# Two MLP layers of a fused attention and MLP kernel: an instruction order written by hand is replaced by one that a list scheduler in the source works out

## The chip, the cores and the metric

One core of one Trainium2 chip runs the whole kernel. The metric is the time of one execution on the device in microseconds (us); the number for a kernel is the median of its runs.

## The reference, cut to what matters

The inputs are float32 arrays: q, k and v of shape (2, 12, 448, 64), and the weights of two MLPs. With `n = 2 * 448 = 896` tokens and a model width of 768 it computes

```
x   = causal_attention(q, k, v)                   # laid out as 896 x 768
x   = (silu(x @ w_gate) * (x @ w_val)) @ w_out    # w_gate, w_val: 768 x 1536
h   = x @ w_in                                    # w_in: 768 x 2048
out = (h * clip(h + 3, 0, 6) / 6) @ w_out2
```

## The kernel before, in words

**The work and its stages.** Four stages follow one another on TensorE: attention, the gate and value layer of the first MLP with its product (here "the f loop"), the layer `w_out` of that MLP, and then the two layers of the second MLP. The weights reach the chip as 64-bit numbers in pairs of 32-bit words, and every 128-column tile of them is turned into float32 on the chip: one ScalarE instruction (`sloped`, line 147) and two on VectorE (`to_float`, line 137: a shift, then an or that joins the low word, which the profile calls TENSOR_SCALAR and SCALAR_TENSOR_TENSOR). Every operand is then split into a high part (a ScalarE copy) and a low part (a subtraction, line 154 for weights, 250 for the tokens), and `mm3` (line 246) makes each product out of three matmuls: high by high, high by low, low by high.

**The f loop.** There are twelve tiles f of 128 columns of `w_gate` and `w_val`. Tile 0 is computed directly for both batches (`first`, line 682, 72 matmuls). Tiles 1 to 11 use seven products instead of eight: each tile's gate and value weights and the two batches of tokens form a 2 by 2 block product in Winograd's scheme. It needs four sums of weight halves (s1 to s4), seven weight pieces, each with its high and low part (a11, s3, s2, s1, a12, a22, s4), the token combinations t1 to t4 made once after attention (line 250), and per f 63 matmuls in seven products in the four PSUM banks x, z, y, w. VectorE joins them with five additions (u2, u3, v2, z, w), ScalarE copies x (p1) and applies Silu twice, and VectorE multiplies gate by value twice (`gate`, line 642). For f below 4 the gated result is split at once; for f from 4 on it is kept in float32 and split later (`halves`, line 669), since no buffers are free until the tokens of attention have been read for the last time.

**What sets the order.** TensorE, VectorE, ScalarE and GpSimd each execute their queue in order. After attention a program-order flag is set for the three vector engines (`on`, line 677) and for TensorE (`on_pe`, line 768); from there to the end of the kernel each engine's queue is the order of the source. That order is written by hand: `chores` (line 722) is a table that says which steps of the next weight tiles stand behind which of the seven products, with special tables for f = 1 and f = 2 and additions for the last f; `slot_work` (line 761) issues them. In the rows of f = 1 the weight tile f + 1 is made whole and tile f + 2 is loaded and turned into float32. The hand-written order also fixes the engine of each subtraction: for f below 3 the low parts of s2, a12 and s4 are on VectorE, all others on GpSimd; the sums s1 and s3 are on GpSimd, s2 and s4 on VectorE; the splits of t3 are on GpSimd, of t2 and t4 on VectorE. The low parts of the `w_out` units (line 158) are on GpSimd, and their loads run two units ahead (line 206). Weight loads go through SyncE's queue into two raw buffers.

Of the kernel before, what the change touches and what calls it, by code (L numbers as in the profile page):

```python
# [23 lines left out]
RAW = 2  # L24
WS = 6
# [5 lines left out]
PLAIN = 1  # L31
EARLY = 4
# [8 lines left out]
class InOrder:  # L41
# [4 lines left out]
    def __getattr__(self, name):  # L46
        call = getattr(self.engine, name)

        def issue(*args, **kw):
            ins = call(*args, **kw)  # L50
            return self.tc.keep_in_program_order(ins) if self.on else ins

        return issue


@with_exitstack
def tile_attention_glu_mlp(
# [517 lines left out]
    def mlps():  # L575
# [13 lines left out]
        (ta, tag_a), (tb, tag_b), (sg, tag_c) = (pair_tile(f"tmp{i}", F32) for i in range(3))  # L589
        s12, tag_s = slot([128, 2, HD, 128], F32, "s12")  # L590

        def operands(f):

            got, fl = {}, {}

            def load(i):
                got["raw", i] = load_raw(cols((w_gate, w_val)[i], f), KD, 128)

            def number(i, step):
                if step == 0:  # L600
                    fl[i] = ring_tile("w", [128, KD, 128], F32, "wgv"[::2][i])
                w = fl[i]
                to_float(w, got["raw", i], (step,))
                fl.update({("a11", "a21")[i]: w[:, :HD], ("a12", "a22")[i]: w[:, HD:]})

            def s1():
                pool.tensor_tensor(out=s12[:, 0], in0=fl["a21"], in1=fl["a22"], op=ALU.add)
                fl["s1"] = s12[:, 0]

            def s3():  # L610
                pool.tensor_tensor(out=fl["a21"], in0=fl["a11"], in1=fl["a21"], op=ALU.subtract)
                fl["s3"] = fl["a21"]

            def s2():
                vec.tensor_tensor(out=s12[:, 1], in0=fl["s1"], in1=fl["a11"], op=ALU.subtract)
                fl["s2"] = s12[:, 1]

            def s4():
                vec.tensor_tensor(out=fl["a12"], in0=fl["a12"], in1=fl["s2"], op=ALU.subtract)
                fl["s4"] = fl["a12"]  # L620

            def piece(name):
                t = got[name] = ring_tile("ws", [128, 2, HD, 128], F32R, name)
                split_w(t[:, 0], t[:, 1], fl[name], vec if f < 3 and name in ("s2", "a12", "s4") else pool)

            todo = {"load1": lambda: load(0), "load2": lambda: load(1)}
            todo.update({n + str(j): lambda i=i, j=j: number(i, j) for i, n in enumerate(("wg", "wv")) for j in (0, 1)})
            todo.update({"s1sum": s1, "s2sum": s2, "s3sum": s3, "s4sum": s4})
            todo.update({n: lambda n=n: piece(n) for n in ("s3", "a11", "s2", "s1", "a12", "a22", "s4")})
            return got, todo  # L630

        def product(ps, a, xk, first, last):
            mm3(
                ps,
                [(a[:, 0, k], a[:, 1, k], t[:, 0], t[:, 1]) for k, (t, _) in enumerate(xk)],
                first=first, last=last, shared=True,
            )

        lent["w"] = [free.pop() for _ in range(W_SLOTS)]
        g1 = {}  # L640

        def gate(f, b, out_ps, in0, in1, step=None):

            whole_f, hi, lo = g1[f]
            if whole_f is not None:
                vec.tensor_tensor(out=whole_f[0][:, BATCH[b]], in0=in0, in1=in1, op=ALU.mult)
                return
            if step != 1:
                vec.tensor_tensor(out=out_ps, in0=in0, in1=in1, op=ALU.mult)
            if step != 0:  # L650
                split(hi[0][:, BATCH[b]], lo[0][:, BATCH[b]], out_ps)

        def g_tiles(f):
            if f < EARLY:
                g1[f] = None, whole(F32R, f"gh{f}"), whole(F32R, f"gl{f}")
            else:
                g1[f] = whole(F32, f"g{f}"), None, None

        ops, todo = {}, {}
        for f in range(PLAIN, K1):  # L660
            ops[f], todo[f] = operands(f)

        def do(f, *names):
            for n in names:
                if f < K1:
                    for part in (n + "0", n + "1") if n in ("wg", "wv") else (n,):
                        todo[f][part]()

        def halves(*fs):
            for f in fs:  # L670
                src, tag = g1[f][0]
                hi, lo = whole(F32R, f"gh{f}"), whole(F32R, f"gl{f}")
                split_w(hi[0], lo[0], src, vec if f < EARLY + 3 or f % 2 else pool)
                g1[f] = None, hi, lo
                free.append(tag)

        on.append(1)
        ws = [made[u] for u in range(2)]
        used[0] += 2
        g_tiles(0)  # L680

        def first(b):

            got = []
            for wh, wl in ws:
                t, n = bank("mm")
                got.append((t[:, :S], n))
                mm3(
                    got[-1][0],
                    [(wh[:, k], wl[:, k], x1[b][k][0][:, 0], x1[b][k][0][:, 1]) for k in range(KD)],  # L690
                )
            idle.extend(n for _, n in got)
            return [t for t, _ in got]

        got = first(0)
        do(1, "load1", "load2", "wg")
        do(2, "load1")
        for h in range(HD):
            split_x(3, h, pool)
        act.activation(out=sg[:, 0], in_=got[0], func=AF.Silu)  # L700
        do(1, "wv")
        do(2, "load2")
        do(1, "s1sum", "s3sum")
        for h in range(HD):
            split_x(2, h, vec)
        do(1, "a11", "s2sum")
        for h in range(HD):
            split_x(4, h, vec)
        later = got[1]
        got = first(1)  # L710
        act.activation(out=sg[:, 1], in_=got[0], func=AF.Silu)
        do(1, "s3", "s2", "s1")
        free.extend(x1[1][h][1] for h in range(HD))
        free.extend(tag for _, tag in sums + more_sums)

        b11, b21, b22 = x1[0][:HD], x1[0][HD:], x1[1][HD:]
        t1, t2, t3, t4 = ([xs[k, h] for h in range(HD)] for k in (1, 2, 3, 4))

        def give(*lists):
            free.extend(tag for l in lists for _, tag in l)  # L720

        def chores(f):

            n = f + 1
            if f == 1:
                return {
                    0: [(1, "a12"), (2, "wg"), (3, "load1")],
                    1: [(1, "s4sum", "a22", "s4"), (2, "wv"), (3, "load2")],
                    2: [(2, "s1sum", "s3sum", "a11")],
                    3: [(2, "s2sum", "s3", "s2"), lambda: gate(0, 0, later, later, sg[:, 0], 0)],  # L730
# [194 lines left out]
```

## Time and profile before

| what | value |
|---|---|
| median of 3 runs | 628.6 us (628.02 to 628.69) |
| the profiled execution | 629.06 us, its span 627.3 us |
| attention, first matmul of the f loop at | 118.26 us |
| f = 1 starts, the layer `w_out` starts | 134.43 us, 302.42 us |
| last two layers | to the end of the span |

The page gives the busy time of each engine over the span, and the span in forty slices with each engine's busy tenths and TensorE's granted clock. A timeline row gives start, duration, engine, instruction, and in brackets how long the engine had stood idle and which instruction released it. "mm" is a PSUM bank, "a" and "s" are weight pieces, "t" token combinations, "x" the tokens, "w" and "v" the float32 gate and value tiles, "tmp" the buffers for u2, u3, v2, p1 and the Silu results. Almost every instruction stands on line 50, the helper that sets the program order, so rows are told apart by tile.

### The profile page before, as it was taken

What the parts mean: (1) busy time and instruction counts of PE and PEld (TensorE: products, weight loads), DVE (VectorE), ACT (ScalarE), POOL (GpSimd) and SP (SyncE); (2) the same over time, 40 slices, a digit from 0 to 9 for tenths busy, and PEclk for the clock granted to TensorE, in tenths of its full rate; (3) what the DMA queues carried; (4) which work ended last, traced back from release to release, by engine and by line L of the source; (5) the groups of instructions that cost most, each with busy time, mean ns of one, the idle gap of its engine ahead of it and who ended that gap; (6) DMA issues with size and microseconds to landing.
All of it is one profiled execution on the core that took longest, in us unless ns stands there. A gap on an engine that the chain in (4) does not pass through costs nothing.

```text
span 627.3 us, 9422 instructions
## 1 busy us (share of the span) xinstructions
PE 598.3 (95%) x3519; PEld 551.8 (88%) x3519; DVE 380.4 (61%) x713; ACT 289.6 (46%) x522; POOL 277.3 (44%) x214
## 2 busy tenths in 40 slices
PE   8999999987598999998999999999999999999997
PEld 5999999876477899998888889998889999999997
DVE  6888999897888777755753333455555556215201
ACT  5687778573544445434533223454555553213200
POOL 4566675274567887873323222222232224213300
PEclk9999999999999999999799999999999999999999
DMA  9555545243343433323134333333334346515102
GB/s 181 131 132 134 133 102 149 78 123 101 106 147 109 143 100 101 115 88 99 52 101 150 101 101 100 101 100 102 102 111 134 107 106 197 151 64 175 53 0 89
DMA packets 83920, 70.16 MB, mean 112 GB/s; under 512 B 35233, under 2 KB 79777, under 8 KB 83873
## 3 DMA queue, kind: packets, MB, share of 16 engines
q1 hardware_dynamic: 83872, 69.55, 38.4%
q8 instruction: 28, 0.46, 0.3%
q14 instruction: 20, 0.16, 0.1%
HBM read 61.73 MB, written 2.75 MB: 103 GB/s over the span
## 4 chain that ended last, share of the span: by engine, by line
PE 70%; DVE 13%; POOL 7%; issue 4%; ACT 4%; DMA 0%; SPq 0%; POOLq 0%; DVEq 0%; ACTq 0%
PE mm L50 56%; PE pv L480 5%; PE sc L409 4%; POOL s L50 4%; PE tp L452 3%; DVE w L50 3%; DVE v L50 3%; POOL a L50 2%; DVE mm L50 1%; PE tr L334 1%; DVE tmp L50 1%; POOL v L50 1%; DVE s L50 1%; ACT w L50 1%; DVE e L422 1%
## 5 line engine op out<-in xcount | busy, mean ns | idle before, releaser
L50 POOL TENSOR_TENSOR wlo<-w,whi 128x768 fp32r<-128x768 f32 (+1 forms) x47 | 85.7, 1824 | 232.5 <-ACT whi L50 199.1
L50 ACT CAST whi<-w 128x768 fp32r<-128x768 f32 (+1 forms) x47 | 38.6, 821 | 99.7 <-DVE w L50 92.6
L50 PE MATMUL mm<-whi,g2l 128*128 128x384 f32 x224 | 74.8, 334 | 0.0
L50 PE MATMUL mm<-whi,g2h 128*128 128x384 f32 x224 | 74.8, 334 | 0.0
L50 PE MATMUL mm<-wlo,g2h 128*128 128x384 f32 x224 | 74.8, 334 | 0.0
L480 PE MATMUL pv<-v,et 112*112 112x65 f32 x480 | 73.5, 243 | 0.8 <-DVE et L458 0.8
L50 DVE TENSOR_SCALAR w<-w 128x768 uint32<-128x768 uint32 (+1 forms) x58 | 50.8, 876 | 38.3 <-ACT w L50 36.0
L50 PE MATMUL mm<-x2h,wlo 128*128 128x384 f32 (+1 forms) x192 | 69.9, 364 | 0.0
L50 PE MATMUL mm<-x2l,whi 128*128 128x384 f32 (+1 forms) x192 | 69.8, 364 | 0.0
L50 PE MATMUL mm<-x2h,whi 128*128 128x384 f32 (+1 forms) x192 | 69.6, 362 | 0.0
L480 PEld LDWEIGHTS pv<-v,et 112*112 112x112 f32 x480 | 65.5, 177 | 2.2 <-DVE et L458 1.0
L50 PE MATMUL mm<-t,s 128*128 128x448 f32 x297 | 62.6, 366 | 2.8 <-DVE gl L50 1.8
L452 PE MATMUL tp<-ident,e 112*112 112x112 f32 x240 | 61.1, 260 | 2.3 <-ACT e L432 2.2
L50 PEld LDWEIGHTS mm<-t,s 128*128 128x128 f32 x297 | 55.6, 188 | 8.2 <-DVE gl L50 2.2
L432 ACT ACTIVATE e<-e,m 112x336 f32<-112x336 f32 (+1 forms) x96 | 48.7, 530 | 20.9 <-DVE m L422 20.6
L50 DVE SCALAR_TENSOR_TENSOR w<-raw,w 128x768 uint32<-128x768 uint32 (+1 forms) x58 | 57.0, 983 | 1.9
L50 PE MATMUL mm<-gl,whi 128*128 128x384 f32 (+1 forms) x144 | 52.9, 367 | 0.0
L50 PE MATMUL mm<-gh,wlo 128*128 128x384 f32 (+1 forms) x144 | 52.9, 367 | 0.0
L50 PE MATMUL mm<-gh,whi 128*128 128x384 f32 (+1 forms) x144 | 52.7, 366 | 0.0
L50 ACT ACTIVATE w<-raw 128x768 f32<-128x768 f32 (+1 forms) x58 | 51.6, 890 | 0.7 <-DMA raw<-in_moe_w_out_dram 0.7
L50 PE MATMUL mm<-x,a 128*128 128x448 f32 x198 | 44.2, 367 | 3.8 <-ACT tmp L50 2.0
L50 PEld LDWEIGHTS mm<-x,a 128*128 128x128 f32 x198 | 37.0, 188 | 7.6 <-ACT tmp L50 2.4
(119 smaller groups left out, 1312.3 us busy)
## 6 DMA issues: line engine op xcount, KB each, us to landing
raw<-in_moe_w_out_dram SPq DMA_DIRECT2D x28, 768.0 KB, 4.3
raw<-in_moe_w_in_dram SPq DMA_DIRECT2D x16, 768.0 KB, 4.5
raw<-in_moe_w_gate_dram SPq DMA_DIRECT2D x12, 768.0 KB, 4.2
raw<-in_moe_w_val_dram SPq DMA_DIRECT2D x12, 768.0 KB, 4.3
kn<-in_k_dram SPq DMA_DIRECT2D x24, 112.0 KB, 2.8
qn<-in_q_dram SPq DMA_DIRECT2D x24, 112.0 KB, 2.8
v<-in_v_dram SPq DMA_DIRECT2D x12, 224.0 KB, 3.2
out_dram<-ob SPq DMA_DIRECT2D x14, 192.0 KB, 1.8
```

The lines of the kernel that those rows point to most:

```text
L50: ins = call(*args, **kw)
L334: nc.tensor.transpose(tr[:, c * C : (c + 1) * C], n[:, c].rearrange("p j d -> p (j d)"), ident[:C, :C])
L409: nc.tensor.matmul(sp[:C, o : o + w], t["qq"][:, j, c * C : (c + 1) * C], t[("kk", "k2")[i]][:, j, 0:w], start=(i == 0), stop=(i == 1),)
L422: nc.vector.tensor_tensor_reduce(out=es, in0=sp[:C, o : o + w], in1=mask[:, S - w :], op0=ALU.add, op1=ALU.min, scale=-SCALE, scalar=3.0e3 ...
L432: nc.scalar.activation(out=es, in_=es, func=AF.Exp, scale=-1.0, bias=m[:, x : x + 1])
L452: nc.tensor.transpose(tp[:C, at - lo : at - lo + C], e[:, at : at + C], ident[:C, :C])
L480: nc.tensor.matmul(box["o"][:, qc, :], et[:, at : at + C], vt[:, j, c, :], start=(c == 0), stop=(c == qc))
```

## The change

The table of chores is gone. The f loop, the splits of the gated results, the layer `w_out` and the weights of the first two units after it are written down as operations of a `Plan`, each with a cost per engine in microseconds and with what it reads and writes, buffers included. `Plan.run` gives each operation a due time, worked backwards from a TensorE that never waits, and then places them: at each step the engine that can start earliest takes, among the operations ready for it, the one due first. TensorE's and SyncE's order stays that of the source. The result is the order in which the instructions are issued. The sums s1 to s4 and the low parts of weight pieces, of token combinations and of the late gated results may go to VectorE or GpSimd, whichever the plan finds free first; the low parts of the `w_out` units are on VectorE alone. Program order is enforced from plan time 9 (TensorE 15), and the flags are cleared behind the plan, so the last two layers are ordered by the framework's own scheduler. The numbers of matmuls, of conversions, of splits and of loads are unchanged. The core of the diff (removed lines left out except in `gate`):

```diff
 PLAIN = 1
+PINNED = 9.0
+START = {"act": 5.6, "vec": 7.9, "pool": 7.0, "pe": 0.0, "sp": 0.0}
+LAG = {"act": 0.15, "vec": 0.15, "pool": 0.15, "pe": 0.25, "sp": 2.4}
 EARLY = 4
...
+class Spot:
+    def __init__(self, make=None, place=None, real=None, ready=0.0):
+        self.make, self.place, self.real, self.ready, self.after = make, place, real, ready, set()
...
+class Plan:
+    def __init__(self):
+        self.ops, self.uses, self.on_place = [], {}, {}
+    def op(self, where, call, reads=(), writes=()):
+        i, before, ready = len(self.ops), set(), 0.0
+        for writing, spots in ((False, reads), (True, writes)):
+            for s in spots:
+                spot, part = s if isinstance(s, tuple) else (s, None)
+                if spot not in self.uses:
+                    self.uses[spot] = []
+                    old = self.on_place.get(spot.place)
+                    if old is not None:
+                        spot.after = {j for _, j, _ in self.uses[old]}
+                    if spot.place is not None:
+                        self.on_place[spot.place] = spot
+                before |= spot.after
+                ready = max(ready, spot.ready)
+                for p, j, w in self.uses[spot]:
+                    if (w or writing) and (p is None or part is None or p == part):
+                        before.add(j)
+                self.uses[spot].append((part, i, writing))
+        before.discard(i)
+        self.ops.append((where, call, before, ready))
+    def run(self, emit):
+        ops, n = self.ops, len(self.ops)
+        after = [[] for _ in range(n)]
+        for i, (_, _, before, _) in enumerate(ops):
+            for j in before:
+                after[j].append(i)
+        clock = 0.0
+        due = [None] * n
+        for i, (where, _, _, _) in enumerate(ops):
+            if "pe" in where:
+                due[i] = clock
+                clock += where["pe"]
+        for i in reversed(range(n)):
+            for j in after[i]:
+                t = due[j] - min(c + LAG[e] for e, c in ops[i][0].items())
+                due[i] = t if due[i] is None else min(due[i], t)
+            if due[i] is None:
+                due[i] = clock
+        left = [len(ops[i][2]) for i in range(n)]
+        at = [ops[i][3] for i in range(n)]
+        free_at = dict(START)
+        pe_order = [i for i in range(n) if "pe" in ops[i][0]]
+        sp_order = [i for i in range(n) if "sp" in ops[i][0]]
+        waiting = {i for i in range(n) if not left[i]}
+        placed = []
+        while waiting:
+            best = None
+            for e in free_at:
+                if e in ("pe", "sp"):
+                    line = pe_order if e == "pe" else sp_order
+                    mine = [line[0]] if line and line[0] in waiting else []
+                else:
+                    mine = [i for i in waiting if e in ops[i][0]]
+                if not mine:
+                    continue
+                t = max(free_at[e], min(at[i] for i in mine))
+                i = min((i for i in mine if at[i] <= t), key=lambda i: (due[i], i))
+                key = (t, due[i], ops[i][0][e], i, e)
+                if best is None or key < best:
+                    best = key
+            t, _, cost, i, e = best
+            waiting.discard(i)
+            free_at[e] = t + cost
+            if e in ("pe", "sp"):
+                (pe_order if e == "pe" else sp_order).pop(0)
+            placed.append((t, len(placed), i, e))
+            for j in after[i]:
+                left[j] -= 1
+                at[j] = max(at[j], t + cost + LAG[e])
+                if not left[j]:
+                    waiting.add(j)
+        assert len(placed) == n
+        for t, _, i, e in sorted(placed):
+            emit(t, e, ops[i][1])
+        self.placed = sorted(placed)
...
+        def parts_of(src, hi, lo, size, both=True):
+            (s, s_part, s_ap), (h, h_part, h_ap), (l, l_part, l_ap) = src, hi, lo
+            plan.op(
+                {"act": 0.1 + size * 0.00098},
+                lambda e: e.copy(h_ap(h()), s_ap(s())), reads=[(s, s_part)], writes=[(h, h_part)],
+            )
+            where = {"vec": 0.08 + size * 0.0012}
+            if both:
+                where["pool"] = 0.1 + size * 0.0027
+            plan.op(
+                where,
+                lambda e: e.tensor_tensor(
+                    out=l_ap(l()), in0=s_ap(s()), in1=h_ap(h()).bitcast(F32), op=ALU.subtract
+                ),
+                reads=[(s, s_part), (h, h_part)], writes=[(l, l_part)],
+            )
...
+        def gate(f, b, bank_, in0, in1):
 
             whole_f, hi, lo = g1[f]
+            mid = lambda t: t[:, BATCH[b]]
+            m = {"vec": 0.63}
             if whole_f is not None:
-                vec.tensor_tensor(out=whole_f[0][:, BATCH[b]], in0=in0, in1=in1, op=ALU.mult)
+                combine(m, at(whole_f, b, mid), in0, in1, ALU.mult)
                 return
-            if step != 1:
-                vec.tensor_tensor(out=out_ps, in0=in0, in1=in1, op=ALU.mult)
-            if step != 0:
-                split(hi[0][:, BATCH[b]], lo[0][:, BATCH[b]], out_ps)
...
+            s1, s2 = at(s12, 0, nth(0)), at(s12, 1, nth(1))
+            either = {"vec": 0.65, "pool": 1.2}
+            out = {}
+            def piece(name, src):
+                t = ring_spot("ws", [128, 2, HD, 128], F32R, name)
+                parts_of(src, at(t, 0, nth(0)), at(t, 1, nth(1)), HD * 128)
+                out[name] = t
+            combine(either, s1, a21, a22, ALU.add)
+            piece("a11", a11)
+            combine(either, a21, a11, a21, ALU.subtract)
+            piece("s3", a21)
+            combine(either, s2, s1, a11, ALU.subtract)
+            piece("s2", s2)
+            piece("s1", s1)
+            piece("a12", a12)
+            combine(either, a12, a12, s2, ALU.subtract)
+            piece("a22", a22)
+            piece("s4", a12)
+            return out
...
+            products(x, a["a11"], b11, True)
+            plan.op(
+                {"act": 0.54}, lambda e, x=x: e.copy(p1[2](ta()), tok(x())), reads=[x], writes=[p1[:2]]
+            )
+            products(z, a["s3"], tk[3], True)
+            products(y, a["s2"], tk[2], True)
+            combine(add, u2, Y, p1, ALU.add)
+            combine(add, u3, Z, u2, ALU.add)
+            products(w, a["s1"], tk[1], True)
+            combine(add, v2, W, u3, ALU.add)
+            products(x, a["a12"], b21, False)
+            silu(at(sg, 0, nth(0)), x)
+            products(z, a["a22"], tk[4], False)
+            combine(add, Z, Z, u2, ALU.add)
+            gate(f, 0, z, Z, at(sg, 0, nth(0)))
+            products(w, a["s4"], b22, False)
+            combine(add, W, W, u2, ALU.add)
+            silu(at(sg, 1, nth(1)), w)
+            gate(f, 1, w, v2, at(sg, 1, nth(1)))
+            idle.extend((nx, ny, nz, nw))
...
+        later = [unit(units[used[0] + i][0]) for i in range(AHEAD)]
+        by = {"act": act, "vec": vec, "pool": pool, "pe": ten, "sp": nc.sync}
+        def emit(t, engine, call):
+            if t >= PINNED and not on:
+                on.append(1)
+            if t >= PINNED + 6 and not on_pe:
+                on_pe.append(1)
+            call(by[engine])
+        plan.run(emit)
+        on.clear()
+        on_pe.clear()
+        made.extend((hi(), lo()) for hi, lo in later)
...
```

## Rows read from the trace of the kernel before

**Rows 1.** The profile's page: engine totals and forty slices of the span

```profile
PE 598.3 (95%) x3519; PEld 551.8 (88%) x3519; DVE 380.4 (61%) x713; ACT 289.6 (46%) x522; POOL 277.3 (44%) x214
...
PE   8999999987598999998999999999999999999997
...
PEclk9999999999999999999799999999999999999999
```

**Rows 2.** Waits of TensorE's matmuls, 118 to 300 us: total, times, longest

```profile
PE mm L50 <- DVE tmp L50: 10.6, 6, 3.1
...
PE mm L50 <- ACT gh L50: 2.7, 1, 2.7
...
PE mm L50 <- POOL a L50: 1.7, 1, 1.7
```

**Rows 3.** Windows of seven of the f tiles: length, busy us (instructions), granted clock

```profile
134.43:155.06 20.63, 13.83 (x64) 11.52 (x63) 17.48 (x24) 9.14 (x18) 11.67 (x11) 1.00 0.39 125
...
155.06:177.23 22.17, 15.20 (x65) 12.77 (x63) 18.84 (x24) 9.11 (x18) 11.66 (x11) 0.92 0.40 124
...
177.23:192.06 14.83, 13.21 (x64) 11.75 (x63) 11.91 (x15) 7.12 (x15) 11.07 (x10) 1.00 0.42 135
...
192.06:206.89 14.83, 13.09 (x64) 11.76 (x63) 11.83 (x15) 6.95 (x14) 11.06 (x10) 1.00 0.34 106
...
220.35:233.31 12.96, 12.96 (x65) 11.76 (x64) 9.92 (x13) 6.18 (x12) 10.93 (x10) 1.00 0.38 121
...
272.49:285.26 12.77, 12.77 (x64) 11.83 (x63) 5.32 (x9) 4.50 (x10) 8.90 (x9) 1.00 0.00 1
...
285.26:302.42 17.16, 14.63 (x64) 13.09 (x63) 10.57 (x13) 8.45 (x12) 4.77 (x3) 0.88 0.32 102
```

**Rows 4.** Timeline of TensorE: start, us, what, [idle before <- releaser]

```profile
153.13 2.09 PE L50 MATMUL mm<-x,s 128*128 128x448 f32 x9 [2.74 <-ACT gh L50]
...
298.90 3.73 PE L50 MATMUL mm<-x,s 128*128 128x448 f32 x9 [2.53 <-DVE tmp L50]
...
302.42 0.52 PE L50 MATMUL mm<-gh,whi 128*128 128x384 f32 x1
...
305.22 0.34 PE L50 MATMUL mm<-gh,whi 128*128 128x384 f32 x1
```

**Rows 5.** Timeline of VectorE at the start of f = 1

```profile
127.79 1.51 DVE L50 TENSOR_SCALAR w<-w 128x768 uint32<-128x768 uint32 x1
...
129.33 1.80 DVE L50 SCALAR_TENSOR_TENSOR w<-raw,w 128x768 uint32<-128x768 uint32 x1
...
131.05 0.55 DVE L50 TENSOR_SCALAR v<-v 128x768 uint32<-128x768 uint32 x1
...
131.63 0.96 DVE L50 SCALAR_TENSOR_TENSOR v<-raw,v 128x768 uint32<-128x768 uint32 x1
...
132.51 3.32 DVE L50 TENSOR_TENSOR t<-xa,t 128x448 fp32r<-128x448 f32 x3
...
141.56 0.55 DVE L50 TENSOR_TENSOR a<-w,a 128x384 fp32r<-128x384 f32 x1
...
146.89 1.28 DVE L50 TENSOR_TENSOR tmp<-mm,tmp 128x448 f32<-128x448 f32 x2
...
151.84 0.62 DVE L50 TENSOR_TENSOR mm<-mm,tmp 128x448 f32<-128x448 f32 x1
...
152.38 0.61 DVE L50 TENSOR_TENSOR tmp<-mm,tmp 128x448 f32<-128x448 f32 x1
```

**Rows 6.** Timeline of GpSimd at the start of f = 1

```profile
126.24 4.08 POOL L50 TENSOR_TENSOR t<-xa,t 128x448 fp32r<-128x448 f32 x3 [0.67 <-ACT t L50]
...
140.19 1.03 POOL L50 TENSOR_TENSOR a<-v,a 128x384 fp32r<-128x384 f32 x1 [0.85 <-ACT a L50]
```

**Rows 7.** Timeline of VectorE ahead of the last product of f = 11

```profile
296.27 2.04 DVE L50 TENSOR_TENSOR gl<-g,gh 128x896 fp32r<-128x896 f32 x1 [1.80 <-ACT gh L50]
...
298.23 0.61 DVE L50 TENSOR_TENSOR tmp<-mm,tmp 128x448 f32<-128x448 f32 x1
```

More of the change, by code (lines that the diff above doesn't have):

```diff
@@ L632, in product, with spot, here @@
[L632 to L636, printed above, removed]
-            )
+        plan = Plan()
+        PE448, PE384, PE512 = 0.2005, 0.1735, 0.2275
+        def spot(place, shape, dt, name):
+            pool_, tag = place
+            return Spot(lambda: pool_.tile(shape, dt, tag=tag, name=name), place)
+        def here(tile_and_place, ready=0.0):
+            real, place = tile_and_place
+            s = Spot(place=place, real=real, ready=ready)
+            plan.uses[s] = []
+            plan.on_place[place] = s
+            return s
@@ new lines, in combine, with at, nth @@
+        def combine(where, out, in0, in1, op):
+            o, a, b = out, in0, in1
+            plan.op(
+                where,
+                lambda e: e.tensor_tensor(out=o[2](o[0]()), in0=a[2](a[0]()), in1=b[2](b[0]()), op=op),
+                reads=[a[:2], b[:2]], writes=[o[:2]],
+            )
+        def at(spot_, part=None, ap=lambda t: t):
+            return spot_, part, ap
+        def nth(i):
+            return lambda t: t[:, i]
+        x1s = [[here(x1[b][k], 6.5 if (b, k) == (1, KD - 1) else 0.0) for k in range(KD)] for b in range(B)]
@@ L639, in mlps @@
+        t1 = [here(xs[1, h], 2.0) for h in range(HD)]
+        xa = [here(sums[h], 7.8 if h == HD - 1 else 0.0) for h in range(HD)]
+        xb = [here(more_sums[h], 7.8 if h == HD - 1 else 0.0) for h in range(HD)]
+        temps = [take([128, 2, S], F32, f"tmp{i}") for i in range(3)]
+        ta, tb, sg = temps
+        s12 = take([128, 2, HD, 128], F32, "s12")
         lent["w"] = [free.pop() for _ in range(W_SLOTS)]
         g1 = {}
-        def gate(f, b, out_ps, in0, in1, step=None):
+        def gate(f, b, bank_, in0, in1):
@@ L663, in do @@
[L663 to L675, printed above, removed]
@@ L805, in mlps @@
-            slot_work(plan, 5)
-            product(w, a["s4"], b22, False, True)
-            add(z, z, u2)
-            gate(f, 0, z, z, sg[:, 0])
-            slot_work(plan, 6)
-            idle.extend((nx, ny, nz))
-            last = finish
-        last()
-        give(b21, b22, t4)
-        free.extend([tag_a, tag_b, tag_c, tag_s] + lent.pop("w"))
-        halves(*range(EARLY + 3, K1))
-        x2 = [(whole(F32R, f"x2h{e}")[0], whole(F32R, f"x2l{e}")[0]) for e in range(KD)]
+            (x, nx), (z, nz), (y, ny), (w, nw) = (bank_spot() for _ in range(4))
```

296 lines of the change are left out of this document (137 added, 159 removed).

## The prediction, made before the changed kernel ran

> **What bounds the kernel now.** I read the page first: TensorE is busy for 95% of the span, and the slices, 15.7 us each, show where the other 5% lies: below 9 tenths are the ninth to eleventh slice (125 to 172 us), the thirteenth and the nineteenth, apart from the launch at the start [rows 1]. Everything behind them runs at 9 tenths or more. All of these lie in the f loop. So the matmuls bound the kernel, except in that loop, which is the part that the change reorders. The waits of the matmuls there say that most of the lost time is ended by VectorE (10.6 us by the additions into tmp), the rest by ScalarE and GpSimd in pieces of 2 to 3 us [rows 2]. A wait alone doesn't say whether VectorE was overloaded or served something else first, so the third view is a table of windows, one per f [rows 3]. It is the view that the sum rests on.
>
> The shortest f, f = 10, takes 12.77 us with TensorE busy throughout: that is the floor of 63 matmuls. The eleven tiles from 134.43 to 302.42 take 167.99 us; eleven floors are 11 x 12.77 = 140.5. The excess is **27.5 us**: 7.9 at f = 1, 9.4 at f = 2, 2.1 at f = 3 and again at f = 4, 0.7 at f = 5 (from 206.89 to 220.35, between two of the rows), 1.1 over f = 6 to 10 (five of them, first and last shown, 64.9 us from 220.35 to 285.26), and 4.4 at f = 11. Behind f = 11 the first nine matmuls of w_out, from 302.42 to 305.22, take 0.31 us each, and their length then falls from 0.52 to 0.34 [rows 4]: the slice that holds them shows a granted clock of 0.7 [rows 1], so part of it at the lower level of 1.2 GHz, and TensorE had stood idle for 2.53 us just before. A matmul of 448 columns takes 12.77 / 63 = 0.203 at f = 10, so one of 384 some 0.174, and 9 x 0.137 = **1.2 us** more are lost here. In all 28.7 us could be won, and no more.
>
> **The change part by part.** It neither adds nor removes matmuls, conversions, splits or loads; it changes who goes first and which of two engines takes a subtraction.
>
> *f = 1 and f = 2 (17.3 us of excess).* Two rows show that order is at fault at least in part. The last product of f = 1 waits 2.74 us, until 153.13 [rows 4]. The row names ScalarE's gh, but that product goes into the bank that v2 reads, and v2 stood in VectorE's queue at 152.38 behind the gate of f = 0 at 151.84 [rows 5], whose bank nobody needs before f = 2; and GpSimd held the low part of a11, the first operand of f = 1, behind two sums, which is the wait of 1.7 us [rows 2]. But VectorE is also nearly full: 17.48 of 20.63 us and 18.84 of 22.17 us [rows 3]. So I count the work that has to be done from 127.8, when attention leaves VectorE free, to the second product of f = 3. Weight tiles of f = 1, 2, 3 into float32: six times 0.55 + 0.96 (at 131.05 and 131.63 [rows 5]) = 9.1 us, VectorE only. Additions, gates and gate splits that read PSUM: 10 additions, 4 + 4 + 2 others, 20 at about 0.6 (two in 1.28 at 146.89 [rows 5]) = 12 us, VectorE only. Subtractions that may go to either engine: 9 for the tokens, 11 each for f = 1 and 2, 4 for f = 3, that is 35, at 0.55 on VectorE (at 141.56 [rows 5]) or 1.03 on GpSimd (at 140.19 [rows 6]). Taking 17 on VectorE (9.4) and 18 on GpSimd (18.5), VectorE has 30.5 us of its own.
>
> The two engines are not independent, as the two timelines show side by side [rows 5, 6]. At 132.51 three subtractions took 3.32 us on VectorE, 1.1 each and twice the 0.55, while GpSimd worked; the shift took 1.51 instead of 0.55 beside GpSimd's three at 126.24, and the or 1.80 instead of 0.96 [rows 5, 6]. The two additions from PSUM at 146.89 kept to 0.64 each although GpSimd worked beside them. So I let GpSimd's 18.5 us pass free beside the 12 us of PSUM work and charge the other 6.5 to VectorE: 37 us. From 127.8 that ends at 164.8; the floor puts the second product of f = 3 at 134.43 + 2 x 12.77 + 1.83 = 161.8. So 3.0 us stay lost even with perfect packing; for waits on ScalarE between the high and the low part I add 5% of 37, 1.9: **4.9 us stay of 17.3**. Bounds: 3.0, and 10.8 if VectorE's busy time of today stays and only its idle time goes (17.48 + 18.84 - 25.54). I take the lower part since the plan also puts off work: today f = 3 is made whole and f = 4 converted before f = 3 starts, some 7 subtractions and two tiles, 7 us that needn't lie here.
>
> The Trainium skill (SBUF — State Buffer, "Who interferes with whom") says that VectorE and GpSimd share one pair of ports under an exclusive lock, and that the second to start is fully blocked; the lengthened rows above agree, the or and GpSimd's own lengthened rows less cleanly. By that rule alone VectorE's 18.5 us of conversions and subtractions and GpSimd's 18.5 us could not overlap at all; with the 12 us from PSUM, under which GpSimd can work, the window would still take the same 37 us, but every meeting of the two in the wrong order would be paid in addition.
>
> *f = 3 to 5 (4.9 us).* VectorE is busy 11.9 of 14.8 us at f = 3 and f = 4; put-off work lands here and the gate splits go on to f = 3. With three low parts less on GpSimd the locked time shrinks by about 3 x (1.03 - 0.55). I leave **1.5** (0 to 4.9).
>
> *f = 6 to 10 (1.1 us).* At 13.0 us per f today, with VectorE at 9.9 and GpSimd at 10.9 [rows 3], there is nothing to win and something to lose: **0.7** stays (0 to 5, see the third rival).
>
> *f = 11 (4.4 + 1.2 us).* The last product waits for v2, which VectorE starts at 298.23 behind a split of 2.04 us that the hand order put ahead [rows 7]. The plan has v2 due before the splits of g6 to g11, whose readers come two units of w_out later, 14 us. **1.0** stays (0 to 5.6).
>
> *Loads, w_out, the last layers.* The loads keep their order on SyncE and their two buffers; the first one of f = 1 is issued during attention's tail as before, so 0. The twelve low parts of w_out units move to VectorE, 1.0 us each by twice 0.55, in a stage of some 86 us in which VectorE is less than half busy: 0. The last two layers lose their fixed order; today their matmuls run without a gap, so nothing can be gained, and I take 0 (up to 2 us lost).
>
> Sum: 4.9 + 1.5 + 0.7 + 1.0 = 8.1 stay of 28.7, **20.6 us go**. The profiled execution took 629.06, 0.46 above the median; 628.6 - 20.6 = **608.0 us**.
>
> **The rivals.** *Work-bound start (0.24).* Only the idle time of VectorE goes: f = 1 and 2 keep 10.8, the rest as above: 14.0 stay, 14.7 go, **614 us**. For it: the lengthened rows, since the plan's costs know nothing of them and give GpSimd work whenever it is free. Against: the 7 us put off. *Near the floor (0.13).* The start ends at its lower bound of 3.0 and the rest at no loss: 25.7 go, **603 us**. Against: f = 6, in a steady state with VectorE idle for 3 us, still loses 0.2 [rows 3]. *A lock in every f (0.11), the slower side.* GpSimd takes a low part at its planned 1.14 us just ahead of the shift or the or, VectorE's queue stands, and u3 or v2 behind it is late in every f; such lengthened conversions stand in [rows 5]. Its price is that of f = 3 and 4 today, 2.06 us. It decides once VectorE's time, blocked time included, passes the 12.8 us of an f: today's 9.9 plus three subtractions moved from GpSimd make 11.6. If f = 1 and 2 stay as they are and f = 3 to 11 all take 14.83, the loop is 42.8 + 9 x 14.83 = 176.3, 8.3 more than now less 1.2 of clock: **636 us**. The same page of the Trainium skill bears on it: the one that starts first decides who is blocked, and the plan's costs have no such term. *Nothing changes (0.04).* The fixed start times of the plan don't fit the machine, an engine waits in order for a raw tile, and what f = 11 gains f = 1 loses: 628.6.
>
> **How the numbers follow.** My forecast has 0.48. Forecast, work-bound start and most of the floor case make 0.8 together; with the last layers' 2 us and the 4 us on either side of the work-bound start the range is 602 to 618. Within 0.2% (1.3 us, about what a measurement here can tell): 0.04; slower 0.11; faster 0.85.
>
> **What would show it.** In the windows by f, f = 1 and 2 near 15 us, f = 3 to 10 at 12.8 to 13.2, f = 11 at 13 to 14; waits of matmuls on tmp down from 10.6 to some 4 us; w_out at full clock from its first matmul. GpSimd should do fewer and VectorE more subtractions from f = 3 on. Wrong if VectorE is busy for over 12 us of each f and the matmuls wait for it there, if f = 1 and 2 still take 35 us or more, or if gaps appear behind the layer w_out.

## The result and the profile after

The changed kernel takes **610.3 us** (median of 4 runs, 609.7 to 611.2) against 628.6: a ratio of 0.971, with a 95% interval of 0.969 to 0.973. The forecast was 608.0. The profiled execution has a span of 608.5 us, 18.8 less than before. Of these, 17.7 were won between the start of f = 1 and the start of w_out (167.99 before, 150.25 after), 1.2 in the layer w_out, and nothing in the last two layers (236.46 us from their first matmul to the end before, 236.47 after, so clearing the order flags neither cost nor gave anything); 0.15 went the other way ahead of f = 1.

The page, engine totals and slices (15.2 us each now):

```profile
PE 595.2 (98%) x3519; PEld 551.1 (91%) x3519; DVE 382.1 (63%) x741; ACT 293.6 (48%) x530; POOL 246.8 (41%) x194
...
PE   8999999997999999999999999999999999999997
...
PEclk9999999997999999999999999999999999999999
```

The section on the change and the prediction say that the number of splits is unchanged. It is not: each of the eight late gated results g4 to g11 is split in two pieces of 384 and 512 columns instead of one of 896, which is 8 more copies on ScalarE (522 to 530) and 8 more subtractions (927 to 935 instructions on VectorE and GpSimd together).

The holes of [rows 1] are gone but for one slice, the tenth (137 to 152 us), which has 7 tenths and is also the only one with a lowered clock (the first and the last slice, the start and the end of the kernel, are below 9 tenths in both kernels). The waits of the matmuls in the f loop, which were some 20 us before, are three single events:

```profile
PE mm L53 <- ACT s L53: 2.1, 1, 2.1
...
PE mm L53 <- DVE s L53: 1.4, 1, 1.4
...
PE mm L53 <- DVE tmp L53: 1.0, 1, 1.0
```

The 10.6 us on tmp [rows 2] have become 1.0. The windows by f, in the columns of [rows 3] (the five busy times are those of TensorE, its weight loads, VectorE, ScalarE and GpSimd, each with its number of instructions):

```profile
134.58:153.91 19.33, 15.87 (x64) 13.52 (x63) 18.50 (x25) 11.95 (x23) 13.69 (x11) 0.82 0.47 156
...
153.91:166.93 13.02, 13.02 (x64) 11.82 (x63) 12.05 (x19) 8.46 (x16) 8.32 (x9) 1.00 0.36 121
...
166.93:179.95 13.02, 13.02 (x64) 11.82 (x63) 11.61 (x17) 6.87 (x13) 7.16 (x7) 1.00 0.38 123
...
179.95:192.97 13.02, 13.02 (x64) 11.82 (x63) 12.34 (x19) 7.85 (x15) 9.55 (x8) 1.00 0.37 121
...
219.01:232.02 13.01, 13.01 (x65) 11.75 (x63) 11.90 (x16) 7.21 (x13) 8.51 (x8) 1.00 0.53 173
...
232.02:246.08 14.06, 13.03 (x65) 11.76 (x63) 13.99 (x18) 7.23 (x13) 11.47 (x9) 1.00 0.55 168
...
272.06:284.83 12.77, 12.77 (x64) 11.84 (x63) 11.93 (x14) 10.93 (x21) 9.11 (x6) 1.00 0.19 63
```

Against [rows 3], f = 1 went from 20.63 to 19.33 us, f = 2 from 22.17 to 13.02, f = 3 and 4 from 14.83 to 13.02 each, f = 11 from 17.16 to 12.77. The f that got clearly dearer is f = 8, from 12.95 (a window of the kernel before that is not among those rows) to 14.06; f = 10 went from 12.77 to 13.14. In f = 8 VectorE is busy for 13.99 us, and the addition u3 came 1.03 us late, behind an or of 1.66 us beside which GpSimd worked:

```profile
242.32 2.09 PE L53 MATMUL mm<-t,a 128*128 128x448 f32 x9 [1.03 <-DVE tmp L53]
...
238.79 1.66 DVE L53 SCALAR_TENSOR_TENSOR v<-raw,v 128x768 uint32<-128x768 uint32 x1
...
236.56 3.06 POOL L53 TENSOR_TENSOR s<-s,s 128x384 fp32r<-128x384 f32 x2 [0.93 <-ACT s L53]
```

f = 1 holds 6.6 of the 9.8 us that the eleven f still take above their floors. TensorE there (start, us, what, idle before and its releaser):

```profile
134.58 1.98 PE L53 MATMUL mm<-x,a 128*128 128x448 f32 x9
...
138.64 0.91 PE L53 MATMUL mm<-t,s 128*128 128x448 f32 x2 [2.08 <-ACT s L53]
...
140.93 7.56 PE L53 MATMUL mm<-t,s 128*128 128x448 f32 x25 [1.38 <-DVE s L53]
```

Two idle times of 2.08 and 1.38 us, and then 25 matmuls in 7.56 us, 0.30 each instead of 0.20: the window shows a granted clock of 0.82, so TensorE ran at the lower level of 1.2 GHz for part of them. What it waited for stands in the rows of ScalarE and of VectorE:

```profile
136.35 1.28 ACT L53 ACT_TABLE_LOAD   x1
...
137.65 0.54 ACT L53 ACTIVATE tmp<-mm 128x448 f32<-128x448 f32 x1
...
138.09 0.50 ACT L53 CAST s<-v 128x384 fp32r<-128x384 f32 x1
```

```profile
135.84 1.36 DVE L53 TENSOR_TENSOR v<-w,v 128x384 f32<-128x384 f32 x1
...
137.13 1.48 DVE L53 TENSOR_TENSOR s<-s,s 128x384 fp32r<-128x384 f32 x1
...
139.53 1.35 DVE L53 TENSOR_TENSOR s<-v,s 128x384 fp32r<-128x384 f32 x1
```

The high part of s3 (138.09, s<-v) stands behind the load of the Silu table and behind the Silu of f = 0, whose result nobody needs soon. In the kernel before the same load was over at 128.5. On VectorE the subtraction that makes s3 (135.84) takes 1.36 us instead of 0.55, until 137.2; so some 0.9 of the 2.08 us are the load and the Silu, and 0.8 are the lengthened subtraction. The low part of s3 (139.53, 1.35 us) stands behind one of s1 (137.13, 1.48 us) and others; the list counts 0.54 for each low part.

### The profile page after: what moved, and what is told of

Same layout as the page of the kernel before. It is cut to its first block, busy times and chain, and to the rows that moved or that the text cites. A ratio compares the mean times of both kernels' runs of the same rounds, so it can differ in the third digit from the quotient of the medians.

```text
span 608.5 us, 9429 instructions
## 1 busy us (share of the span) xinstructions
PE 595.2 (98%) x3519; PEld 551.1 (91%) x3519; DVE 382.1 (63%) x741; ACT 293.6 (48%) x530; POOL 246.8 (41%) x194
## 4 chain that ended last, share of the span: by engine, by line
PE 80%; DVE 12%; POOL 3%; issue 2%; ACT 1%; DMA 0%; SPq 0%; DVEq 0%; ACTq 0%; POOLq 0%
PE mm L53 65%; PE pv L580 5%; PE sc L509 4%; PE tp L552 3%; DVE w L53 2%; DVE v L53 2%; POOL s L53 1%; DVE s L53 1%; PE tr L434 1%; DVE tmp L53 1%; POOL a L53 1%; DVE e L522 1%; DVE qq L447 1%; PE tr L614 1%; DVE mm L53 1%
## 5 line engine op out<-in xcount | busy, mean ns | idle before, releaser
L53 POOL TENSOR_TENSOR wlo<-w,whi 128x768 fp32r<-128x768 f32 (+1 forms) x33 | 59.4, 1801 | 243.9 <-PE mm L53 219.6
L53 DVE TENSOR_SCALAR w<-w 128x768 uint32<-128x768 uint32 (+1 forms) x58 | 39.7, 685 | 79.3 <-ACT w L53 78.7
L53 PE MATMUL mm<-t,s 128*128 128x448 f32 x297 | 65.6, 378 | 3.5 <-ACT s L53 2.1
L53 PEld LDWEIGHTS mm<-t,s 128*128 128x128 f32 x297 | 57.5, 194 | 9.9 <-ACT s L53 2.5
L53 DVE SCALAR_TENSOR_TENSOR w<-raw,w 128x768 uint32<-128x768 uint32 (+1 forms) x58 | 59.7, 1029 | 0.9
L522 DVE CUSTOM_DVE_ANT_0 e<-sc,mask 112x336 f32<-112x336 f32 (+1 forms) x96 | 40.7, 445 | 4.5 <-PE sc L509 2.6
```

The source lines that it names most:

```text
L522: nc.vector.tensor_tensor_reduce(out=es, in0=sp[:C, o : o + w], in1=mask[:, S - w :], op0=ALU.add, op1=ALU.min, scale=-SCALE, scalar=3.0e3 ...
```

## The experiments

The same base kernel ran beside each group of runs (628.7 to 629.1 us). Ratios are to it.

**e1: the scheduler's order, but the engines of the kernel before.** Each subtraction gets one engine instead of a choice, the one that it had:

```diff
-            where = {"vec": 0.08 + size * 0.0012}
-            if both:
-                where["pool"] = 0.1 + size * 0.0027
+            where = {side: 0.08 + size * 0.0012 if side == "vec" else 0.1 + size * 0.0027}
```

> The changed kernel with its scheduler, but every subtraction may go only to the engine that the kernel before gave it. If the gain comes from the order (theory 1), most of it stays: f = 1 gets dearer because nine of its subtractions go back to GpSimd at 1.0 to 1.4 us, f = 11 and the put-off work stay won: 612 to 616 us. If the free choice of the engine is what wins (theory 2), at least half of the 18.4 us comes back: 620 us or more, with VectorE near 9.9 us and GpSimd near 11 us in each f.

Measured 613.0 us (0.974, interval 0.972 to 0.976). f = 1, 2 and 6 in the columns above:

```profile
134.24:155.23 20.99, 16.02 (x65) 13.97 (x63) 19.58 (x27) 11.48 (x21) 12.31 (x11) 0.84 0.40 130
...
155.23:168.00 12.77, 12.77 (x65) 11.83 (x63) 11.39 (x17) 7.32 (x14) 8.94 (x8) 1.00 0.40 124
...
207.62:221.79 14.17, 13.03 (x65) 11.75 (x63) 13.76 (x15) 7.45 (x14) 13.84 (x12) 1.00 0.53 167
```

Theory 1 holds: **about 16 of the 18.4 us come from the order alone**, and the free choice of engines adds some 2 (2.7 by the times, 1.6 by the ratios, whose intervals overlap). f = 1 got dearer, as expected; its 20.99 us are no better than the 20.63 of the kernel before, so the order wins nothing there and everything behind it. The shorter pieces of the late splits are kept in e1; how much of f = 11 and `w_out` is theirs was not tested. With the old engines f = 2 to 4 run at the floor, and f = 5 to 7 wait about a microsecond each for an addition on VectorE, which is busy for 13.8 of 14.2 us.

**e2: everything on VectorE.** GpSimd gets no sum and no low part of the f loop or of the late splits:

```diff
-            if both:
+            if False:
...
-            either = {"vec": 0.65, "pool": 1.2}
+            either = {"vec": 0.65}
```

> The changed kernel with all sums and low parts of the f loop on VectorE; GpSimd has no work there. If VectorE and GpSimd together are needed (theory 1), VectorE has 3.0 of conversions, 5.5 of additions and gates and 11 x 0.5 of subtractions, 14.0 us in an f of 12.8: 1.2 more for each of ten f and a dearer start, 622 to 630 us. If GpSimd's help is worth nothing because it lengthens VectorE's instructions as much as it takes off (theory 2), the time stays within 3 us of 610, with the conversions back at 0.55 and 0.96 us.

Measured **605.5 us** (0.962, interval 0.960 to 0.964), 4.8 us below the change. Theory 1, which the prediction's count implies, falls; the time is also 1.5 us below the 607 of theory 2, so GpSimd's help was worth less than nothing. f = 1, 2, 3 and 9:

```profile
134.25:147.02 12.77, 12.77 (x64) 11.82 (x63) 12.19 (x23) 5.51 (x11) 0.00 (x0) 1.00 0.21 70
...
147.02:161.23 14.21, 13.22 (x64) 11.68 (x63) 13.80 (x27) 8.29 (x16) 0.00 (x0) 1.00 0.36 122
...
161.23:174.99 13.76, 13.23 (x64) 11.68 (x63) 13.21 (x26) 7.93 (x16) 0.00 (x0) 1.00 0.38 126
...
241.73:254.50 12.77, 12.77 (x65) 11.83 (x64) 11.77 (x23) 6.16 (x12) 0.00 (x0) 1.00 0.38 120
```

f = 1 is at the floor, and in f = 9 VectorE does all 11 subtractions, the conversions, additions and gates in 11.77 us. TensorE loses 0.6 to 1.4 us at each of f = 2 to 5, where the gates are also split and VectorE is busy for 12.8 to 13.8, 0.4 at f = 6, and 1.0 at f = 8, where VectorE has no more to do than in f = 9. In f = 2 to 5 and 8 the wait is for the high part of s3, which stands in ScalarE's queue behind a conversion that waited 0.4 us (f = 8: 1.9) for its weight load; so VectorE need not be the only cause there. Its instructions at the end of f = 1 show why it fits:

```profile
142.46 0.56 DVE L53 TENSOR_SCALAR w<-w 128x768 uint32<-128x768 uint32 x1
...
142.93 0.55 DVE L53 TENSOR_SCALAR v<-v 128x768 uint32<-128x768 uint32 x1
...
143.40 0.95 DVE L53 SCALAR_TENSOR_TENSOR w<-raw,w 128x768 uint32<-128x768 uint32 x1
...
144.27 0.62 DVE L53 TENSOR_TENSOR tmp<-mm,tmp 128x448 f32<-128x448 f32 x1
...
144.80 0.55 DVE L53 TENSOR_TENSOR s<-w,s 128x384 fp32r<-128x384 f32 x1
...
145.27 0.95 DVE L53 SCALAR_TENSOR_TENSOR v<-raw,v 128x768 uint32<-128x768 uint32 x1
```

With GpSimd idle the shift takes 0.55 and the or 0.95. Read by their starts (142.46, 142.93, 143.40, 144.27, 144.80, 145.27) they follow one another at 0.47 for a shift, 0.87 for the or, 0.53 for an addition and 0.47 for a subtraction, less than the length of their rows: each row starts before the one ahead of it has ended.

**e3: the kernel before, only the tail of f = 11 reordered.** The splits of g4 and a prefetch go behind v2:

```diff
-                for i in (1, 3, 5):
+                for i in (1, 4, 5):
...
-                plan[3] += [lambda: give(b11, t3), lambda: halves(EARLY)]
+                plan[4] += [lambda: give(b11, t3), lambda: halves(EARLY)]
```

> The kernel before, with one edit in the last f: the first splits of g4 and the prefetch of a w_out unit stand behind v2 instead of ahead of it. If f = 11 was lost to the order of that one addition, its 17.16 us become 13 to 14 and w_out starts at full clock: 623 to 625 us. If VectorE is short of time there, v2 is in time but the gates or the splits behind it are late instead: 627 to 629 us.

Measured 631.0 us (1.002, interval 1.001 to 1.004), 2 us above the range of the second theory: nothing won, and the second theory's mechanism holds. TensorE from the last product of f = 11 into w_out:

```profile
298.26 1.99 PE L50 MATMUL mm<-x,s 128*128 128x448 f32 x9
...
304.03 0.44 PE L50 MATMUL mm<-gh,whi 128*128 128x384 f32 x1 [1.18 <-ACT gh L50]
...
306.09 0.69 PE L50 MATMUL mm<-gl,whi 128*128 128x384 f32 x1 [1.62 <-DVE gl L50]
...
307.32 0.63 PE L50 MATMUL mm<-gl,whi 128*128 128x512 f32 x1
```

The 2.5 us of waiting for v2 are gone, and f = 11 takes 12.78 us. But the same splits are now late for w_out: it waits 1.18 us for a high and 1.62 for a low part of g, runs at the lower clock behind that (0.63 us long matmuls of 512 columns), and takes 93.3 us instead of 88.4: the 4.4 us are given back. In this run f = 6 to 9 also took 13.6 us instead of 13.0, which the edit doesn't explain. So it was not the place of that one addition alone that was at fault in f = 11: the splits, the conversions and v2 all have to find their place, which the list does (12.77 us, and no wait in w_out).

**e4: the kernel before, work put off by hand.** In f the tile f + 1 is converted and split, and nothing of f + 2 (the new table, for f from 3 on):

```diff
-                0: [(n, "a11"), (n + 1, "wg"), (n + 2, "load1")],
-                1: [(n, "s3"), (n + 1, "wv"), (n + 2, "load2")],
...
+                0: [(n, "wg"), (n + 1, "load1")],
+                1: [(n, "wv"), (n + 1, "load2")],
+                2: [(n, "s1sum", "s3sum", "a11")],
+                3: [(n, "s2sum", "s3")],
```

> The kernel before, still ordered by hand and with its engines, but the weight tiles are made one f later (tile f + 1 is converted and split during f, nothing of f + 2) and the gates of f = 0 stand two products later in f = 1. If putting off work is most of what f = 1 and f = 2 win (theory 1), their 42.8 us become 34 to 38 and the time 620 to 624 us. If it needs the scheduler's fine order (theory 2), f = 1 and f = 2 stay at 41 to 44 us, or later f get slower since their weights come late: 627 to 640 us.

Measured 643.7 us (1.022, interval 1.021 to 1.024), 3.7 above the range of theory 2. f = 1, 2 and 6:

```profile
134.47:154.56 20.09, 13.84 (x65) 11.52 (x64) 16.69 (x22) 7.74 (x16) 11.33 (x10) 1.00 0.39 125
...
154.56:173.65 19.09, 15.43 (x65) 13.75 (x63) 12.06 (x19) 8.49 (x17) 8.11 (x8) 0.82 0.27 83
...
221.56:236.67 15.11, 13.30 (x65) 11.68 (x63) 8.86 (x13) 6.23 (x13) 9.27 (x10) 1.00 0.37 113
```

f = 1 and 2 together fall from 42.8 to 39.2 us, so putting work off wins 3.6 there. Most later f take 15.1 to 15.3 us (f = 4 even 19.3, f = 5 13.4), since two conversions stand in VectorE's queue ahead of u3, and f = 11 takes 21.2, where v2 comes 5.3 us late behind a conversion and a split. Theory 2: the later start of the weights alone, in this one table, loses more behind f = 2 than it wins; the order within an f has to go with it.

**e5: e2, with GpSimd at work on nothing.** Beside each low part of a weight piece GpSimd subtracts the same operands into a scratch tile:

```diff
+                plan.op(
+                    {"pool": 0.1 + size * 0.0027},
+                    lambda e: e.tensor_tensor(
+                        out=noise, in0=s_ap(s()), in1=h_ap(h()).bitcast(F32), op=ALU.subtract
+                    ),
+                    reads=[(s, s_part), (h, h_part)],
+                )
```

> The kernel with all sums and low parts on VectorE (605.5 us), and beside each of the seven low parts of an f a subtraction of the same operands on GpSimd into a scratch tile that nobody reads. If GpSimd's use of the memory that VectorE reads is itself what costs (theory 1), VectorE's subtractions grow from 0.55 to 0.8 or more, and its 12 us in an f of 12.8 no longer fit: 615 to 640 us. If in the changed kernel it was GpSimd's own slow results that somebody waited for (theory 2), an idle burden changes nothing: 605 to 607 us.

Measured **664.2 us** (1.056, interval 1.052 to 1.059), 59 us above e2 and 24 above the range of theory 1, whose mechanism holds. Nobody reads what GpSimd makes; it does hold its operands for longer, so a part of the 59 us may be buffers that come free late. Two windows there, each from the fifth product of an f to the fifth of the next (f = 3 to 4 and f = 6 to 7), and VectorE's groups from 134 to 300 us:

```profile
182.42:200.28 17.86, 15.08 (x65) 12.89 (x63) 16.90 (x25) 7.45 (x14) 8.41 (x7) 0.90 0.28 89
...
239.82:258.03 18.21, 15.02 (x65) 12.94 (x63) 16.51 (x23) 6.45 (x12) 8.69 (x7) 0.91 0.27 87
```

```profile
L53 DVE TENSOR_TENSOR a<-w,a 128x384 fp32r<-128x384 f32 x18 | 20.5, 1136 | 0.0
...
L53 DVE TENSOR_TENSOR tmp<-mm,tmp 128x448 f32<-128x448 f32 x27 | 16.7, 617 | 13.2 <-PE mm L53 9.1 <-issue 2.1 <-ACT s L53 2.0
...
L53 DVE SCALAR_TENSOR_TENSOR v<-raw,v 128x768 uint32<-128x768 uint32 x9 | 15.9, 1770 | 0.0
...
L53 DVE TENSOR_TENSOR a<-v,a 128x384 fp32r<-128x384 f32 x9 | 4.9, 543 | 0.0
```

An f takes 18 us, at a granted clock of 0.90, with VectorE busy for 16.5 to 16.9 instead of 11.8 to 13.2. Not every row is longer: the low parts of a11 and a12 (a<-w,a) take 1.14 us instead of 0.55 and the or on v 1.77 instead of 0.95, while the low part of a22 (a<-v,a) keeps 0.54, the or on w 0.95, and the additions that read PSUM 0.62. Added up over all groups of that view, VectorE's rows are some 41 us longer than the same number of rows of e2, beside 63 GpSimd subtractions: **0.65 us each, where the subtraction that GpSimd could take over costs VectorE 0.47**. That is the price where each GpSimd subtraction reads what VectorE reads as well.

In the change, with its own mix of work, price and saving cancel: in f = 7 VectorE is busy for 11.90 us with 16 instructions and GpSimd has 8, and in f = 9 of e2 VectorE does 23 in 11.77. Over f = 2 to 11 it is 123.3 us for 170 instructions in the change and 123.4 for 241 in e2: 71 instructions fewer saved VectorE nothing.

The Trainium skill (SBUF — State Buffer, "Who interferes with whom") states an exclusive lock on a shared port pair for VectorE instructions with two SBUF inputs against GpSimd instructions that read SBUF, and none for at most one SBUF input outside VectorE's two-port modes. The lengthened subtractions, the or and the PSUM additions agree with it. The shift, with one SBUF input, took 1.51 instead of 0.55 beside GpSimd in [rows 5]; no run here shows in which mode it ran.

**e6: e2 with the table loaded early.** One Silu of one column, ahead of the f loop:

```diff
+        warm = const.tile([128, 1], F32, name="warm")
+        nc.scalar.activation(out=warm, in_=x1[1][KD - 2][0][:, 0, 0:1].bitcast(F32), func=AF.Silu)
```

> The same kernel with one ScalarE instruction of one column added before the f loop, so that the 1.28 us of loading the Silu table are over before the high part of s3 of f = 1. In the run with all subtractions on VectorE, VectorE stood idle for 1.23 us behind that load, and was then busy without a gap until f = 2, which came 1.4 us late. If VectorE's backlog is what delays f = 2 and f = 3 (theory 1), 1 us is won: 604 to 605 us. If something else does (the weights' loads, ScalarE's order), nothing: 605 to 606.

Measured 607.7 us (0.967, interval 0.965 to 0.970), 2.3 above e2; both theories miss. The load moved into the end of attention:

```profile
117.12 1.28 ACT L691 ACT_TABLE_LOAD   x1
...
118.53 0.50 ACT L53 CAST whi<-w 128x384 fp32r<-128x384 f32 x1
```

It delays the high part of the first gate tile (118.53), f = 1 starts at 135.63 instead of 134.25, which is 1.4 of the 2.3 us, and f = 2 still takes 14.55 us. The load has no free place where I put it.

**e7: the change, TensorE kept busy.** Twenty matmuls into the bank z, which the next product overwrites:

```diff
+            if f == 1:
+                def fill(e, t=z, a=a["a11"]):
+                    for _ in range(20):
+                        e.matmul(
+                            tok(t()), a()[:, 0, 0], b11[0]()[:, 0], start=True, stop=True, skip_group_check=True
+                        )
+                plan.op({"pe": 0.01}, fill, reads=[a["a11"], b11[0]], writes=[z])
```

> The changed kernel, with twenty matmuls of no use between the first and the second product of f = 1, where TensorE waits 3.5 us. If the slower matmuls behind that wait (27 in 8.3 us instead of 5.6) are the lower clock after an idle TensorE, they go and f = 1 falls from 19.3 to about 16.5 us: 607 to 608 us. If they are slow since their operands arrive late, nothing changes or the twenty matmuls come on top: 610 to 613 us.

Measured 608.3 us (0.968, interval 0.967 to 0.970), 0.3 above the range given for the lower clock:

```profile
134.05 6.04 PE L53 MATMUL mm<-x,a 128*128 128x448 f32 x29
...
139.93 5.92 PE L53 MATMUL mm<-t,s 128*128 128x448 f32 x27
```

The 27 matmuls of s3, s2 and s1 take 5.76 us from start to start of the next product, and f = 1 falls to 17.13. So they were slow for the clock and not for their operands, and the lower clock after 3.5 us of idling cost 2 us of the change's time.

**e8, e9: the change, with GpSimd dear.** Twice (e8) and three times (e9) the cost of GpSimd in the list:

```diff
-                where["pool"] = 0.1 + size * 0.0027
+                where["pool"] = 0.2 + size * 0.0054
...
-            either = {"vec": 0.65, "pool": 1.2}
+            either = {"vec": 0.65, "pool": 2.4}
```

> The changed kernel with GpSimd's costs doubled in the scheduler's list, so that it gets a subtraction only where VectorE is behind. If each subtraction on GpSimd costs VectorE more than it saves (theory 1), fewer of them are better: between the 605.5 us of none and the 610.3 of the change. If a few help where VectorE alone is behind, at f = 2 to 5 (theory 2), it beats 605: 602 to 604 us.

> The changed kernel with GpSimd's costs in the list three times those of the change (the run before had twice, 604.0 us with 5 to 6 subtractions on GpSimd in an f). If the optimum lies between some and none (theory 1), three times is about the same or goes up towards the 605.5 us of none: 603 to 605.5. If fewer is always better and only the start needs GpSimd (theory 2), it falls: 601 to 603 us.

e8 measured **604.0 us** (0.961, interval 0.959 to 0.963), 6.3 us below the change and the fastest of all runs; e9 606.2 (0.964, interval 0.962 to 0.967). f = 1, 2, 3 and 10 of e8:

```profile
134.51:148.89 14.38, 13.23 (x65) 11.68 (x64) 14.12 (x23) 9.67 (x18) 4.83 (x4) 1.00 0.32 108
...
148.89:163.15 14.26, 13.21 (x65) 11.67 (x64) 14.26 (x23) 8.51 (x17) 7.82 (x6) 1.00 0.46 143
...
163.15:175.91 12.76, 12.76 (x64) 11.83 (x63) 12.74 (x19) 7.14 (x16) 7.48 (x7) 1.00 0.38 123
...
252.85:265.62 12.77, 12.77 (x65) 11.84 (x64) 11.62 (x19) 7.50 (x13) 5.90 (x5) 1.00 0.45 137
```

Eight of the eleven f run at the floor of 12.77 us; f = 1 and 2 lose 3.1 together, and there is no lowered clock. GpSimd does 4 to 7 subtractions in an f, against 5 to 11 in the change. In e8 theory 2 is met, at the upper edge of its range, and f = 3 to 5, where VectorE alone lost 0.6 to 1.0 us each, are at the floor; but f = 2, which it also names, is no better than in e2 (14.26 against 14.21). In e9 theory 1 is the nearer, though the time lies 0.7 above its range. That the optimum lies between none and the change's share is not shown: of none, twice and three times (605.5, 604.0 and 606.2) each interval overlaps the next. What is clear of noise is that all three lie below the change.

Of the 6.4 us by which the f loop of e8 is shorter than that of the change, 5.0 lie in f = 1 (some 2 of them the clock, by e7) and 1.3 in f = 8; f = 2 takes 1.2 back, and the rest is the slower pace without waits described at the end.

**e10: e8 with VectorE's measured costs.** The costs of shift, or, sums, low parts, additions and gates set to the distances of e2:

```diff
-            plan.op({"vec": 0.75}, shift, writes=[w])
-            plan.op({"vec": 1.15}, join, reads=[raw], writes=[w])
+            plan.op({"vec": 0.50}, shift, writes=[w])
+            plan.op({"vec": 0.95}, join, reads=[raw], writes=[w])
...
-        add = {"vec": 0.63}
+        add = {"vec": 0.56}
```

> GpSimd's costs doubled as in the 604.0 us run, and VectorE's costs in the list set to the distances at which its instructions follow one another when GpSimd is idle (0.50 shift, 0.95 or, 0.50 sums, 0.48 low parts, 0.56 additions and gates). If the list orders better with truer costs (theory 1), the 3.1 us still lost at f = 1 and 2 shrink: 601 to 603.5 us. If the higher costs of the change stand in for the waits on GpSimd that the list doesn't know (theory 2), VectorE is planned too tight and additions come late: 605 to 609 us.

Measured 611.0 us (0.973, interval 0.971 to 0.975). Waits of the matmuls for the additions:

```profile
PE mm L53 <- DVE tmp L53: 4.6, 5, 1.9
```

Theory 2, and worse than expected: additions come late in five places, up to 1.9 us. That the costs that are right for VectorE alone are too low as long as GpSimd shares the work, and that the change's higher ones carry this unstated, fits these waits; which cost does it was not tested.

## Why the prediction was right, and where it was not

The direction, the place and the size held: 608.0 forecast, 610.3 measured, from the f loop alone, by order and not by less work. Term by term, of the 28.7 us that could be won:

- **f = 1 and 2**: 4.9 us were to stay, 6.8 did (19.33 + 13.02 - 25.54). All of it lies in f = 1, where I had expected both near 15. f = 2 went to 13.02 at once. The step that failed is that the count had no term for the clock: the 3.5 us of waiting would have fitted, but the lower clock behind it added the 2 us that e7 took away again. That the rest came near 4.9 is in part luck. The count had VectorE run out of time towards the second product of f = 3, and there, and in all of f = 2, no matmul waits; the waits are for the two parts of s3 at the second product of f = 1, one behind lengthened rows and a table load, one behind other subtractions. And the 1.9 us for waits on ScalarE were taken from no row; the one such wait was 2.08.
- **f = 3 to 5**: 1.5 forecast, 0.75 stayed, none of it a wait: it is the slower pace (13.02 us instead of 12.77). **f = 11 and w_out**: 1.0 forecast, about 0 stayed; e3 shows that this took more than the one addition that I named.
- **f = 6 to 10**: 0.7 forecast, 2.2 stayed, of which 1.3 at f = 8 (14.06 against the floor of 12.77). That is the third rival's mechanism, VectorE full and an addition late behind a lengthened or, in one f instead of nine.
- **The last layers** at 0: they took the same time to 0.01 us. The low parts that moved to VectorE were 14 and not 12, for the two units behind w_out are planned as well.

What the count got wrong without harm to its sum is the part of GpSimd. I let 18 of 35 subtractions go to it, two thirds of them free beside PSUM work, and took each instruction at the length of its row and not at its distance to the next. By the rows VectorE alone needs 9.1 + 12 + 35 x 0.55 = 40.4 us, more than the 37 of the count; by the distances of e2 it needs, as an estimate, 6 x (0.47 + 0.87) + 20 x 0.53 + 35 x 0.47 = 35.1, and e2 does lose only 1.4 us at f = 1 and 2. e2 and e5 show that VectorE does all of them in the same time, and that a subtraction on GpSimd beside it takes as much from VectorE as it gives (the change) or more (e5). GpSimd did not do many fewer subtractions either, 7 to 9 in each of f = 2 to 9 against 10 or 11. The gain came from which instruction stands first (e1), and the choice of engines at these costs, which was the other half of the change, holds back some 6 us (e8), most of them in f = 1.

In e8 f = 1 still waits 1.15 us for the high part of s3, again behind the table load and the Silu of f = 0, and f = 2 waits 1.05 us for u3; no run has both gone. Still open is why a list with truer costs does worse by 7 us: e10 shows late additions, but not which cost makes them late.

## What to carry to other kernels

Where VectorE's queue decides when the matmuls go on, work out which of its instructions is due next and let that order it: one addition moved by hand only passed the wait on (e3), and a later start of the weights by hand did the same (e4). Before a second engine is given a share, measure what it takes from the first: keep it busy on nothing and read the other's rows. And read the cost of a pipelined instruction from start to start.

## What the runs showed of the hardware that was not expected

A GpSimd subtraction of 384 columns on the operands that VectorE uses lengthened VectorE's rows by 0.65 us, more than the 0.47 that the same subtraction costs there (e5); in the change, beside a mix of work, 78 subtractions on GpSimd in f = 2 to 11 saved VectorE no time. TensorE's products went at two paces without any wait or lowered clock: an f of 63 matmuls took 13.02 us in f = 2 to 6 of the change and 12.77 in its f = 11, in most f of e8 and in several of e7. What switches between them these runs don't tell; over the change's f loop it makes some 1.5 us.
